# Last expert's sends behind the branch around the overflow part, its second products block by block, its last copy halved

## The chip, the cores and the metric

The kernel runs on one core of a Trainium2 chip. TensorE (PE) multiplies matrices, VectorE (DVE), ScalarE (ACT) and GpSimd (POOL) do the rest, SyncE (SP) issues most loads; POOL issues the indirect DMAs that scatter rows. The metric is the device time of one execution in microseconds (us). Before the change three runs took 419.87, 419.90 and 421.45 us, a median of 419.9 us.

## The reference, cut to what matters

```python
def _moe_ref(x, w_gate, w_output_gate, w1, w2):        # x: 3072 x 512, the output of the attention part
    e_idx = np.argmax(x @ w_gate, axis=1)              # one of 8 experts for each token
    ...                                                # gate_w: softmax; eom: sigmoid of x @ w_output_gate
    for e in range(E):
        mask = e_idx == e
        h = np.maximum(x[mask] @ w1[e], 0.0)           # 512 -> 1024
        ye = h @ w2[e]                                 # 1024 -> 512
        out[mask] = gate_w[mask, None] * eom[mask, e, None] * ye
```

Ahead of it stands a causal linear attention with decay (4 batches, 8 heads, 768 steps), whose output is x. All values are float32; the kernel splits each matrix into a high and a low part and does three products for one.

## The kernel before, in words

The first third (to about 150 us) computes the attention in chunks of 128 steps, picks each token's expert and scatters the tokens' rows, sorted by expert, into a buffer `srt` in device memory. Then the experts are worked through in order of their number of tokens. Each has a fixed room for tokens (`CAPS`, 448 down to 368). Tokens that do not fit, should there be any, are done at the end in the overflow part, which stands inside a branch, `tc.If(odd > 0)`. In the inputs at hand the count is zero and the branch jumps over it.

The work on experts is a loop over steps `s`, eight steps (slices of 128 of the 1024 hidden columns) to an expert; `NS` is 64. A step does the first product `mm1(s)` into a PSUM tile `h` (line 985; 12 matmuls, in one of four arms of a small branch, by the expert's size), then ACT and DVE make the two parts `hh` and `hl` of its relu (lines 994, 995), and the second product of the step before is added into four PSUM tiles `a`.

The last expert is different: its second product is turned round (`stage2_last`, line 1036), so that tokens lie on the partitions of the result. It has three blocks of tokens `tb` (128, 128 and 112), three matmuls of 512 columns for each block and step, and one PSUM tile for each block. When a block has all eight steps, `emit_last` (lines 1039 to 1049) copies it out of PSUM into `orow`, by ACT for blocks 0 and 2 and by DVE for block 1, and POOL sends it to the rows of `out` that `idl` names (`send`, line 215). `idl` holds the token numbers, made in step 61 by three small DVE operations.

The order of the instructions on each engine is the order in which the code is written (`manual_schedule`), up to `order_ctx.close()`. Behind it come the overflow part and the end of the program. Each of the five engines has its own copy of the branch: it loads the count `n_odd` (line 1117), compares and jumps (line 1143). Where the body is skipped, an engine runs a short other arm, which waits until its earlier work is complete and raises its semaphores by what the body would have raised. On POOL that arm waits for all its DMAs and then does one operation on the semaphores of the DMA queue, shown as INC_SWDGE_SEM. The end of the program (line 1254) is a chain of waits on SP, a DRAIN on each engine and a meeting of all engines.

Of the kernel before, what the change touches and what calls it, by code (L numbers as in the profile page):

```python
# [10 lines left out]
F32 = mybir.dt.float32  # L11
F32R = mybir.dt.float32r
BF16 = mybir.dt.bfloat16
I32 = mybir.dt.int32
# [19 lines left out]
def retention_moe_kernel(  # L34
# [14 lines left out]
    nc = tc.nc  # L49
    P = 128  # L50
    HP = P // 2
    B, H, S, D = q.shape
    E, DM, DF = w1.shape
    NT = B * S
# [4 lines left out]
    NF = DF // P  # L59
# [3 lines left out]
    NTB = math.ceil(CAPS[-1] / P)  # L63
# [3 lines left out]
    cpool = ctx.enter_context(tc.tile_pool(name="cpool", bufs=1))  # L67
    wpool = ctx.enter_context(tc.tile_pool(name="wpool", bufs=8))
    hpool = ctx.enter_context(tc.tile_pool(name="hpool", bufs=1))
# [8 lines left out]
    order_ctx = ExitStack()  # L78
    order_ctx.enter_context(tc.manual_schedule())

    def fill_up(pool, n):

        return pool.tile([P, n], F32, name="fill")
# [36 lines left out]
    iof = cpool.tile([P, E], F32, name="iof")  # L120
    ck = cpool.tile([P, E], F32, name="ck")
    arm = cpool.tile([P, E], I32, name="arm")
    fill_up(cpool, 24)

    def constants_first():

# [87 lines left out]
    def send(dst, idx, src, n):  # L214
        st = nc.gpsimd.indirect_dma_start(  # L215
            out=dst, out_offset=bass.IndirectOffsetOnAxis(ap=idx, axis=0),
            in_=src, in_offset=None, bounds_check=n - 1, oob_is_err=False)

        tc.declare_no_dep(st.ins, group="out", reason="rows are disjoint")
        tc.add_to_no_dep_group("out", st.ins)  # L220
# [17 lines left out]
    with ExitStack() as actx:  # L238
# [651 lines left out]
        run_head(12)  # L890
        split_low(NF - 1, None, nc.vector)

    with ExitStack() as mctx:
        mp = mctx.enter_context(tc.tile_pool(name="mp", bufs=2))
        NS = E * NF
# [140 lines left out]
                nc.tensor.matmul(accs[tb][0:w.stop - w.start], l[:, w], r[:, 1], start=(f == 0 and n == 0),  # L1036
                                 stop=(f == NF - 1 and n == 2))

        def emit_last(tb):
            n = min(P, CAPS[-1] - tb * P)  # L1040
            orow = mp.tile([P, DM], F32, name="orow", tag="orow", bufs=NTB)

            src = accs[tb][0:n].rearrange("p (dc a j) -> p dc a j", a=4, j=32)
            dst = orow[0:n].rearrange("p (a dc j) -> p dc a j", a=4, j=32)
            if tb % 2 == 0:
                nc.scalar.copy(dst, src)
            else:
                nc.vector.tensor_copy(dst, src)
            send(out, idl[0:n, tb:tb + 1], orow[0:n], NT)

        def load_idl(e):
            m = mp.tile([P, NTB], F32, name="idm", tag="idm", bufs=1)
# [1 line left out]
            return m  # L1054

        def round_idl(m):
            t = mp.tile([P, NTB], I32, name="idl", tag="idl", bufs=1)
            tmp = mp.tile([P, NTB], I32, name="tmpl", tag="tmpl", bufs=1)
            token_ids(t, m, slotl, ck[:, E - 2:E - 1], tmp, True)
            return t  # L1060

        arms = {}

# [20 lines left out]
        for s in range(NS + 1):  # L1084
            e, f = divmod(s, NF)
            if f == 0 and 1 <= e < E - 1:
                load_rank(e + 1)
            while loaded < min(NS, s + NF + 1):
                load_weights(loaded)
                loaded += 1  # L1090
            if f == 1 and e + 1 < E:
                load_x(e + 1)
            while split < min(NS, s + NF - 1):
                split_weights(split)
                split += 1
            first_mm = [lambda C: mm1(s, C)] if s < NS else []
            second_mm = [lambda C: mm2(s - 1, C)] if 1 <= s <= NS - NF else []
            if f == 0:
                if first_mm:
                    by_size(e, *first_mm)  # L1100
                if second_mm:
                    by_size(e - 1, *second_mm)
            else:
                by_size(e, *first_mm, *second_mm)
            if s < NS:
                relu1(s)
            if second_mm:
                finish(s - 1)
            if e == 0:
                if f >= 1:  # L1110
                    arms[f] = nc.values_load(arm[0:1, f - 1:f], engines=(mybir.EngineType.PE,), min_val=0, max_val=ARMS - 1)
            if NS - NF < s < NS - 1:
                for tb in range(NTB):
                    stage2_last(s - 1, tb)
            elif s == NS:

                odd = nc.values_load(n_odd[0:1, 0:1], min_val=0, max_val=NT + 1)
                for tb in range(2):
                    stage2_last(NS - 2, tb)
                for tb in range(NTB):  # L1120
                    if tb >= 2:
                        stage2_last(NS - 2, tb)
                    stage2_last(NS - 1, tb)
                    emit_last(tb)
            if e == 0:
                head_send(f)
            if f == NF - 1 and 1 <= e + 1 < E - 1:
                clear(e + 1)
            if e >= 1 and s < NS and f >= 1:
                for n in range(2 * f - 2, min(math.ceil(PASS[e - 1][1] / 32), 2 * f)):  # L1130
                    emit(e - 1, n)
            dc = f - (3 if e == 0 else 4)
            if 0 <= dc < NDC and e + 1 < E:
                prep_x(e + 1, dc)
            if s == NS - NF:
                idm = load_idl(E - 1)
            if s == NS - 3:
                idl = round_idl(idm)


    order_ctx.close()

    with tc.If(odd > 0):
        with ExitStack() as octx:
# [4 lines left out]
            def block(r0, e):  # L1149

                xo = op.tile([P, ROW], F32, name="xo", tag="xo")
                nc.sync.dma_start(xo, srt[ds(r0, P), :])
                oi = op.tile([P, 1], I32, name="oi", tag="oi")
                nc.vector.tensor_scalar(out=oi, in0=xo[:, P:P + 1].bitcast(I32), scalar1=-0.25, scalar2=0.25 * KEEP,
                                        op0=ALU.mult, op1=ALU.add)
                xf = op.tile([P, DM], F32, name="xf", tag="xf")
                nc.vector.tensor_copy(xf.rearrange("p (dc a j) -> p dc a j", a=4, j=32),
                                      xo.rearrange("p (a x) -> p a x", x=SEG)[:, :, 0:P].rearrange("p a (dc j) -> p dc a j", j=32))
                pt = psv.tile([P, NDC, P], F32, name="pt", tag="pt")
                for dc in range(NDC):  # L1160
                    nc.tensor.transpose(pt[:, dc], xf[:, dc * P:(dc + 1) * P], ident)
                xt = op.tile([P, NDC, P], F32, name="xto", tag="xto")
                nc.vector.tensor_copy(xt, pt)
                yo = op.tile([P, DM], F32, name="yo", tag="yo")
                ht = op.tile([P, NF, P], F32, name="ht", tag="ht")
                for fg in range(2):
                    wa = op.tile([P, NDC, 512], F32, name="wa", tag="wa")
                    for o in range(2):
                        nc.sync.dma_start(wa[o * HP:o * HP + HP], w1[ds(e, 1), o * DM // 2:(o + 1) * DM // 2, fg * 512:(fg + 1) * 512]
                                          .rearrange("z (dc p) f -> p (z dc) f", p=HP))  # L1170
                    ph = psv.tile([P, 4, P], F32, name="ph", tag="ph")
                    for j in range(4):
                        for dc in range(NDC):
                            nc.tensor.matmul(ph[:, j], wa[:, dc, j * P:(j + 1) * P], xt[:, dc],
                                             start=(dc == 0), stop=(dc == NDC - 1))
                    nc.scalar.activation(ht[:, fg * 4:fg * 4 + 4], ph, AF.Relu)
                po = psv.tile([P, DM], F32, name="po2", tag="po2")
                for fg in range(2):
                    wb = op.tile([P, 4, DM], F32, name="wb", tag="wb")
                    nc.sync.dma_start(wb, w2[ds(e, 1), fg * 512:(fg + 1) * 512, :].rearrange("o (j p) d -> p (o j) d", p=P))  # L1180
                    for j in range(4):
                        nc.tensor.matmul(po, ht[:, fg * 4 + j], wb[:, j], start=(fg == 0 and j == 0),
                                         stop=(fg == 1 and j == 3))
                nc.vector.tensor_copy(yo, po)
                nc.gpsimd.indirect_dma_start(
                    out=out, out_offset=bass.IndirectOffsetOnAxis(ap=oi, axis=0),
                    in_=yo, in_offset=None, bounds_check=NT - 1, oob_is_err=False)

            rows = oc.tile([P, 1], I32, name="rows")
            nc.gpsimd.iota(rows, pattern=[[0, 1]], base=0, channel_multiplier=1)  # L1190
# [17 lines left out]
            for r, cap in enumerate(CAPS + [TOP]):  # L1208
                nov = nc.values_load(over[0:1, r:r + 1], min_val=0, max_val=NT)
                with tc.If(nov > 0):  # L1210
                    e = nc.values_load(order[0:1, r:r + 1], engines=(ET.SP,), min_val=0, max_val=E - 1)
                    clear_from(endk[:, r:r + 1], 0)
                    with tc.For_i(0, nov, P) as t0:
                        block(e * REG + cap + t0, e)


# [42 lines left out]
```

## Time and profile before

| | us |
|---|---|
| median of three runs | 419.9 |
| the profiled execution's own time | 421.54 |
| span of the profiled execution, first to last instruction | 419.6 |
| TensorE busy | 404.4 |
| last matmul starts | 409.35 |
| last send starts on POOL | 411.11 |

The span is the stretch between the first and the last instruction of the trace; the execution's own time lies 1.95 us above it. Start times below count from the start of the span. Names such as POOLq or SPq mean an engine's sequencer, which takes instructions in order, waits on semaphores and jumps; POOL or DVE alone means the engine at work.

### The profile page before, as it was taken

The numbers are of one execution on the slowest core, as the hardware profiler recorded it, in microseconds if no ns is written. First come the engines' busy times: TensorE is split into PE (matmuls) and PEld (weight loads), VectorE is DVE, ScalarE is ACT, GpSimd is POOL, SyncE is SP. The second block draws the span as 40 slices with busy tenths as digits, with TensorE's granted clock in tenths as the row PEclk, the third lists the DMA queues.
The fourth block names the chain that finished last, engine by engine and source line by source line (L and its number), as shares of the span: only waits on it lengthen the run. The fifth ranks groups of instructions, "written<-read, shape, count | busy, mean of one in ns | idle before, by whom it ended". The sixth has DMA issues, their size and how long they took to land.

```text
span 419.6 us, 10492 instructions
## 1 busy us (share of the span) xinstructions
PE 404.4 (96%) x3611; PEld 378.3 (90%) x3611; DVE 222.8 (53%) x557; ACT 185.3 (44%) x360; POOL 257.3 (61%) x306
## 2 busy tenths in 40 slices
PE   7999999999999999999999999999999999999990
PEld 4878887888879999999999999999999999999880
DVE  3355667666687766744543553563555454553120
ACT  2366555555565325634533544443454454452110
POOL 3655664454587127883367777777786787876702
PEclk9899999999999999999999999999999999999996
DMA  8999788988744969797494588469459659620102
GB/s 187 256 240 244 214 232 220 252 204 220 203 141 154 248 147 269 222 211 191 141 224 140 148 200 207 155 180 232 136 172 237 176 168 208 214 75 28 47 3 75
DMA packets 130157, 75.75 MB, mean 181 GB/s; under 512 B 61748, under 2 KB 118216, under 8 KB 130064
## 3 DMA queue, kind: packets, MB, share of 16 engines
q1 hardware_dynamic: 122928, 59.38, 58.1%
q0 software_dynamic: 5904, 15.04, 10.3%
q8 instruction: 61, 1.00, 1.0%
q14 instruction: 32, 0.26, 0.2%
q10 hardware_dynamic: 1232, 0.06, 0.2%
HBM read 59.71 MB, written 15.30 MB: 179 GB/s over the span
## 4 chain that ended last, share of the span: by engine, by line
PE 79%; issue 5%; POOL 5%; DMA 5%; DVE 2%; ACT 1%; SPq 1%; POOLq 0%; ACTq 0%; DVEq 0%
PE h L985 29%; PE a L1008 27%; PE y L411 4%; PE s L393 4%; PE s L353 2%; PE st L418 2%; PE y L385 2%; POOL out_dram L215 2%; PE s L340 2%; PE s L522 1%; DMA qn<-in_q_dram 1%; PE s L622 1%; PE a L1036 1%; DMA raw<-in_moe_w_dram 1%; DMA srt<-row,pos 1%
## 5 line engine op out<-in xcount | busy, mean ns | idle before, releaser
L201 POOL TENSOR_TENSOR wlo<-raw,whi 128x512 fp32r<-128x512 f32 x56 | 74.9, 1338 | 44.3 <-ACT whi L193 27.1
L215 POOL DMA_INDIRECT out_dram<-ot,idi x85 | 84.7, 996 | 22.5 <-issue 17.7
L985 PE MATMUL h<-xh,whi 128*128 128x360 f32 (+5 forms) x256 | 84.3, 329 | 0.1
L985 PE MATMUL h<-xw,whi 128*128 128x360 f32 (+5 forms) x256 | 84.3, 329 | 0.0
L985 PE MATMUL h<-xh,wlo 128*128 128x360 f32 (+5 forms) x256 | 84.2, 329 | 0.0
L995 DVE SCALAR_TENSOR_TENSOR hl<-h,hh 128x192 fp32r<-128x192 f32 (+7 forms) x64 | 35.4, 554 | 82.8 <-ACT hh L994 81.2
L1008 PE MATMUL a<-hh,whi 128*128 128x392 f32 (+4 forms) x224 | 73.8, 329 | 0.0
L1008 PE MATMUL a<-hl,whi 128*128 128x392 f32 (+4 forms) x224 | 73.8, 329 | 0.0
L1008 PE MATMUL a<-hh,wlo 128*128 128x392 f32 (+4 forms) x224 | 73.5, 328 | 0.0
L994 ACT ACTIVATE hh<-h 128x192 fp32r<-128x192 f32 (+7 forms) x64 | 31.2, 488 | 73.5 <-PE h L985 73.5
L192 ACT CAST whi<-raw 128x512 fp32r<-128x512 f32 x64 | 39.6, 618 | 40.9 <-PE a L1008 31.1
L200 DVE TENSOR_TENSOR wlo<-raw,whi 128x512 fp32r<-128x512 f32 x60 | 42.4, 707 | 27.2 <-ACT whi L192 22.9
L985 PEld LDWEIGHTS h<-xh,whi 128*128 128x128 f32 x256 | 48.2, 188 | 0.9 <-issue 0.4
L985 PEld LDWEIGHTS h<-xw,whi 128*128 128x128 f32 x256 | 48.2, 188 | 0.6
L985 PEld LDWEIGHTS h<-xh,wlo 128*128 128x128 f32 x256 | 48.2, 188 | 0.2
L538 POOL DMA_INDIRECT srt<-row,pos x24 | 24.2, 1007 | 38.9 <-ACT row L529 31.2
L401 DVE TENSOR_TENSOR am<-s,mask 128x512 f32<-128x512 f32 x48 | 29.9, 684 | 30.6 <-PE s L393 28.5
L1008 PEld LDWEIGHTS a<-hl,whi 128*128 128x128 f32 x224 | 42.2, 188 | 0.3
L1008 PEld LDWEIGHTS a<-hh,wlo 128*128 128x128 f32 x224 | 42.2, 188 | 0.2
L1008 PEld LDWEIGHTS a<-hh,whi 128*128 128x128 f32 x224 | 42.2, 188 | 0.2
L193 ACT CAST whi<-raw 128x512 fp32r<-128x512 f32 x64 | 39.6, 618 | 1.1 <-DMA raw<-in_moe_w_dram 1.1
L927 ACT CAST xh<-xt 128x416 fp32r<-128x416 f32 (+2 forms) x28 | 15.1, 540 | 36.7 <-DVE xt L926 36.7
(201 smaller groups left out, 642.1 us busy)
## 6 DMA issues: line engine op xcount, KB each, us to landing
raw<-in_moe_w_dram SPq DMA_DIRECT2D x128, 128.0 KB, 4.8
raw<-in_moe_w_dram SPq DMA_DIRECT2D x64, 256.0 KB, 4.1
kn<-in_k_dram SPq DMA_DIRECT2D x24, 256.0 KB, 4.6
vn<-in_v_dram SPq DMA_DIRECT2D x24, 256.0 KB, 5.0
qn<-in_q_dram SPq DMA_DIRECT2D x10, 512.0 KB, 5.6
xl<-srt SPq DMA_DIRECT2D x12, 209.6 KB, 5.5
xl<-srt SPq DMA_DIRECT2D x8, 225.8 KB, 3.3
xl<-srt SPq DMA_DIRECT2D x8, 193.5 KB, 4.8
```

Of the source, the lines that this page charges most:

```text
L192: nc.scalar.copy(hi[:, 0], raw[:, 0])
L193: nc.scalar.copy(perm(hi), r2)
L200: (first or nc.vector).tensor_sub(lo[:, 0], raw[:, 0], hi[:, 0].bitcast(F32))
L201: (second or nc.gpsimd).tensor_sub(perm(lo), r2, perm(hi).bitcast(F32))
L215: st = nc.gpsimd.indirect_dma_start(out=dst, out_offset=bass.IndirectOffsetOnAxis(ap=idx, axis=0), in_=src, in_offset=None, bounds_check=n ...
L393: nc.tensor.matmul(sp[2 * (n % 2) + b][:, (2 * S_ + o) * P:(2 * S_ + o) * P + P], kt[n][rows(b), g], queries(n, g, b), start=True, stop=Tr ...
L401: nc.vector.tensor_tensor(out=a.rearrange("p s o t -> p (s o) t"), in0=sp[2 * (n % 2) + b].rearrange("p (x t) -> p x t", t=P), in1=mask.un ...
L538: s_ = nc.gpsimd.indirect_dma_start(out=srt, out_offset=bass.IndirectOffsetOnAxis(ap=rt.pop(("pos", i)), axis=0), in_=row.rearrange("p a x ...
L985: nc.tensor.matmul(ps[:, 0:C], l[:, 0, w], r[:, dc, 0:C], start=(n == 0), stop=(n == 3 * NDC - 1))
L994: nc.scalar.activation(hh, ps[:, 0:C], AF.Relu)
L995: nc.vector.scalar_tensor_tensor(out=hl, in0=ps[:, 0:C], scalar=0.0, in1=hh.bitcast(F32), op0=ALU.max, op1=ALU.subtract)
L1008: nc.tensor.matmul(accs[d][:, 0:C], l[:, 1, w], r[:, 0:C], start=(f == 0 and n == 0), stop=(f == NF - 1 and n == 2))
```

## The change

The three sends of the last expert move from in front of the branch to behind it: `emit_last` becomes `copy_last`, which only copies and puts the tile on a list `lasts`; the sends are written out after the overflow part. For that `orow` and `idl` move to pools that live to the end (`orow` to the three 2 KB buffers of tag `h0`, which the first expert's head used; `idl` to the constants, with the padding behind it cut from 24 to 16 words). The second products of step 61 no longer run between the first products of steps 62 and 63 but after the latter, together with those of steps 62 and 63, and all of one block of tokens before the next. The copy of the last block is split: ACT copies the first half of its columns, DVE the second. Block 0 stays with ACT and block 1 with DVE. The send inside the overflow part, which is skipped, is written with the helper.

```diff
@@ constants
+    idl = cpool.tile([P, NTB], I32, name="idl")
-    fill_up(cpool, 24)
+    fill_up(cpool, 16)
@@
-        def emit_last(tb):
+        def copy_last(tb):
             n = min(P, CAPS[-1] - tb * P)
-            orow = mp.tile([P, DM], F32, name="orow", tag="orow", bufs=NTB)
+            orow = hpool.tile([P, DM], F32, name="orow", tag="h0", bufs=3)
...
-            if tb % 2 == 0:
+            if tb == 0:
                 nc.scalar.copy(dst, src)
+            elif tb < NTB - 1:
+                nc.vector.tensor_copy(dst, src)
             else:
-                nc.vector.tensor_copy(dst, src)
-            send(out, idl[0:n, tb:tb + 1], orow[0:n], NT)
+                nc.scalar.copy(dst[:, 0:2], src[:, 0:2])
+                nc.vector.tensor_copy(dst[:, 2:4], src[:, 2:4])
+            lasts.append((orow, n))
@@ the loop over steps
-            if NS - NF < s < NS - 1:
+            if NS - NF < s < NS - 2:
                 for tb in range(NTB):
                     stage2_last(s - 1, tb)
             elif s == NS:
                 odd = nc.values_load(n_odd[0:1, 0:1], min_val=0, max_val=NT + 1)
-                for tb in range(2):
-                    stage2_last(NS - 2, tb)
                 for tb in range(NTB):
-                    if tb >= 2:
-                        stage2_last(NS - 2, tb)
-                    stage2_last(NS - 1, tb)
-                    emit_last(tb)
+                    for x in (NS - 3, NS - 2, NS - 1):
+                        stage2_last(x, tb)
+                    copy_last(tb)
@@
-    order_ctx.close()
     with tc.If(odd > 0):
...
+    for tb, (orow, n) in enumerate(lasts):
+        send(out, idl[0:n, tb:tb + 1], orow[0:n], NT)
+    order_ctx.close()
```

On POOL, at the end of its program, the order before was as follows (first the place of the branch, then, after the skipped body, the other arm and the end; `orow` and `idl` are the last expert's rows and token numbers, what stands in square brackets are the semaphores that a row waits for).

```order
L1117 TENSOR_LOAD n_odd [waits DVE_49]
L215 DMA out_dram<-orow,idl 3072x512 [waits DMASW0_49,DVE_49,Activation_49]
L215 DMA out_dram<-orow,idl 3072x512 [waits DMASW1_49,DVE_49]
L215 DMA out_dram<-orow,idl 3072x512 [waits DMASW2_49,Activation_49]
L1143 COMPARE_AND_BRANCH
...
L1143 ISA [waits Pool_49,Pool_sequencer_49,DMASW4_49,DMASW5_49,DMASW3_49,DMASW6_49,DMASW2_49,DMASW7_49,DMASW1_49,DMASW0_49]
L1143 UNCONDITIONAL_BRANCH
L1254 ISA [waits barrier_Pool_Activation_PE_DVE_SP_gather]
```

In the changed program the same place of POOL reads as follows.

```order
L1120 TENSOR_LOAD n_odd [waits DVE_49]
L1141 COMPARE_AND_BRANCH
...
L1141 ISA [waits Pool_49,Pool_sequencer_49,DMASW4_49,DMASW5_49,DMASW3_49,DMASW6_49,DMASW2_49,DMASW7_49,DMASW1_49,DMASW0_49]
L1141 UNCONDITIONAL_BRANCH
L216 DMA out_dram<-orow,idl 3072x512 [waits DMASW0_49,DVE_49,Activation_49]
L216 DMA out_dram<-orow,idl 3072x512 [waits DMASW1_49,DVE_49]
L216 DMA out_dram<-orow,idl 3072x512 [waits DMASW2_49,DVE_49]
L1254 UNCONDITIONAL_BRANCH
L1254 ISA [waits barrier_Pool_Activation_PE_DVE_SP_gather]
```

The three sends have moved past the branch and past the other arm's wait for the DMA queues; one jump to the program's end is new behind them.

On DVE, at the same place, the rows before are these (`hl` is the low part of a step's relu).

```order
L995 SCALAR_TENSOR_TENSOR hl<-h_2651,hh 128x368 [waits Activation_49]
L995 SCALAR_TENSOR_TENSOR hl<-h_2652,hh 128x368 [waits Activation_49]
L1117 TENSOR_LOAD n_odd [waits DVE_49]
L1048 COPY orow<-a_2646 128x4x4x32 [waits PE_49]
L1143 COMPARE_AND_BRANCH
```

And in the changed program:

```order
L997 SCALAR_TENSOR_TENSOR hl<-h_2653,hh 128x368 [waits Activation_49]
L1120 TENSOR_LOAD n_odd [waits DVE_49]
L1050 COPY orow<-a_2647 128x4x4x32 [waits PE_49]
L1053 COPY orow<-a_2648 112x2x4x32 [waits Activation_49]
L1141 COMPARE_AND_BRANCH
```

DVE has one copy more, a half of 256 columns, and it waits for ACT, not for PE: the two halves run one after the other.

## Rows read from the trace of the kernel before

**Rows 1.** The page, part 1: busy time, share and instructions of each engine.
```profile
PE 404.4 (96%) x3611; PEld 378.3 (90%) x3611; DVE 222.8 (53%) x557; ACT 185.3 (44%) x360; POOL 257.3 (61%) x306
```

**Rows 2.** Busy time by stretch: start:end, length, PE, PEld, DVE, ACT, POOL, clock, DMA share.
```profile
core 0: us, PE busy (x) PEld busy (x) DVE busy (x) ACT busy (x) POOL busy (x), PEclk, DMA share, GB/s
405.40:409.80 4.40, 4.34 (x20) 3.13 (x18) 1.23 (x2) 1.09 (x3) 0.97 (x1) 1.00 0.02 6
409.80:419.60 9.80, 0.00 (x0) 0.00 (x0) 0.00 (x0) 0.56 (x1) 1.96 (x2) 0.63 0.23 79
```

**Rows 3.** The chain of waits, end of the span: start, length, what.
```profile
396.65 0.97 POOL out_dram L215
...
409.84 0.62 POOL out_dram L215
410.46 0.65 issue
411.11 0.98 POOL out_dram L215
```

**Rows 4.** The timeline from 405 us: start, length, engine, operation [idle before, releaser].
```profile
405.61 0.48 ACT L994 ACTIVATE hh<-h 128x368 fp32r<-128x368 f32 x1 [3.52 <-PE h L985]
406.12 0.54 DVE L995 SCALAR_TENSOR_TENSOR hl<-h,hh 128x368 fp32r<-128x368 f32 x1 [3.46 <-ACT hh L994]
...
407.70 0.59 ACT L1046 COPY orow<-a 128x512 f32<-128x512 f32 x1 [1.61 <-PE a L1036]
...
408.39 0.69 DVE L1048 COPY orow<-a 128x512 f32<-128x512 f32 x1 [1.73 <-PE a L1036]
...
408.56 0.97 POOL L215 DMA_INDIRECT out_dram<-orow,idl  x1 [10.94 <-ACT orow L1046]
...
409.12 0.39 PE L1036 MATMUL a<-whi,hl 128*112 128x512 f32 x1
409.35 0.39 PE L1036 MATMUL a<-wlo,hh 128*112 128x512 f32 x1
409.78 0.58 ACT L1046 COPY orow<-a 112x512 f32<-112x512 f32 x1 [1.50 <-PE a L1036]
409.84 0.97 POOL L215 DMA_INDIRECT out_dram<-orow,idl  x1 [0.30 <-issue]
411.11 0.98 POOL L215 DMA_INDIRECT out_dram<-orow,idl  x1 [0.30 <-issue]
```

**Rows 5.** Instructions of the branch's line 1143: count, shortest/median/longest ns, first and last start.
```profile
L1143 POOLq EVENT_SEMAPHORE  x6: 17/30/571, 413.3 to 414.3; - x6
L1143 DVEq EVENT_SEMAPHORE  x2: 21/21/21, 411.3 to 411.4; - x2
L1143 ACTq EVENT_SEMAPHORE  x2: 17/17/17, 412.5 to 412.6; - x2
L1143 PEldq COMPARE_BRANCH  x1: 3473/3473/3473, 406.8 to 406.8; - x1
L1143 DVEq COMPARE_BRANCH  x1: 76/76/76, 408.4 to 408.4; - x1
L1143 ACTq COMPARE_BRANCH  x1: 54/54/54, 409.8 to 409.8; - x1
L1143 POOLq COMPARE_BRANCH  x1: 53/53/53, 410.4 to 410.4; - x1
L1143 POOLq INC_SWDGE_SEM  x1: 686/686/686, 415.9 to 415.9; - x1
```

**Rows 6.** The same line, 413.6 to 414.28 us alone: the wait for the third send.
```profile
L1143 POOLq EVENT_SEMAPHORE  x2: 43/307/571, 413.6 to 413.7; - x2
```

**Rows 7.** Instructions of the program's end, line 1254; the last row from 418.79 us alone.
```profile
L1254 SPq EVENT_SEMAPHORE  x14: 17/28/28, 416.5 to 419.5; - x14
L1254 POOLq DRAIN  x3: 46/103/2118, 416.6 to 419.3; - x3
L1254 SPq DRAIN  x3: 7/7/13, 417.3 to 419.0; - x3
...
L1254 POOLq EVENT_SEMAPHORE  x4: 17/17/17, 418.8 to 419.5; - x4
```

**Rows 8.** Copies and the like of 256 or 192 columns on ACT and DVE.
```profile
L442 ACT COPY lt<-misc x12: 368/405/405, 19.4 to 128.3; 128x256 f32<-128x256 f32 x12
L609 DVE SCALAR_TENSOR_TENSOR h<-y,h x7: 415/424/425, 131.8 to 149.7; 128x256 fp32r<-128x256 f32 x7
L995 DVE SCALAR_TENSOR_TENSOR hl<-h,hh 128x192 fp32r<-128x192 f32 x8 | 2.8, 353 | 1.3 <-ACT hh L994 1.1
```

**Rows 9.** The load of the count on POOL, line 1117.
```profile
L1117 POOLq TENSOR_LOAD <-n_odd x1: 506/506/506, 388.7 to 388.7; - x1
```

**Rows 10.** All sends into the output, whole span: time from issue to landing.
```profile
DMA to landing us min/median/max: 2.2/3.8/6.4
```

**Rows 11.** Jumps in the loop over steps, line 969, on PE's sequencer.
```profile
L969 PEldq COMPARE_BRANCH  x186: 65/176/2924, 171.4 to 402.1; - x186
```

More of the change, by code (lines that the diff above doesn't have):

```diff
@@ L891, in retention_moe_kernel @@
         split_low(NF - 1, None, nc.vector)
+    lasts = []
     with ExitStack() as mctx:
@@ L1056, in round_idl @@
         def round_idl(m):
-            t = mp.tile([P, NTB], I32, name="idl", tag="idl", bufs=1)
             tmp = mp.tile([P, NTB], I32, name="tmpl", tag="tmpl", bufs=1)
-            token_ids(t, m, slotl, ck[:, E - 2:E - 1], tmp, True)
-            return t
+            token_ids(idl, m, slotl, ck[:, E - 2:E - 1], tmp, True)
         arms = {}
@@ L1137, in retention_moe_kernel @@
             if s == NS - 3:
-                idl = round_idl(idm)
-    order_ctx.close()
+                round_idl(idm)
     with tc.If(odd > 0):
@@ L1184, in block @@
                 nc.vector.tensor_copy(yo, po)
-                nc.gpsimd.indirect_dma_start(
-                    out=out, out_offset=bass.IndirectOffsetOnAxis(ap=oi, axis=0),
-                    in_=yo, in_offset=None, bounds_check=NT - 1, oob_is_err=False)
+                send(out, oi, yo, NT)
             rows = oc.tile([P, 1], I32, name="rows")
```

## The prediction

> **What bounds the kernel now.** The page's first part comes first: TensorE is busy for 96% of the span [rows 1]. The stretches then show where that ends: to 409.8 us PE has no gap, and in the last 9.8 us it does nothing [rows 2]. The change adds and removes no matmul, so what it can win lies in those 9.8 us. The chain of waits ends in POOL's three sends and says nothing of what follows the last [rows 3]. The timeline shows the approach: three copies out of PSUM, three sends [rows 4]. The rest is found only in the instructions of the branch's line and of the program's end [rows 5 to 7], laid end to end:
>
> - The last matmul's result is ready at 409.78, where ACT's third copy starts; the copy ends at 410.36 [rows 4].
> - The third send could start 0.28 us later (that is the distance at the first: copy to 408.29, send at 408.56 [rows 4]), so at 410.64. It starts at 411.11, since POOL is still at the second; sends stand 1.28 apart. It ends at 412.09 [rows 4].
> - POOL's sequencer, behind the branch, waits for that send's landing until 413.7 + 0.57 = 414.3 [rows 6]. This is 2.2 us behind the send's end, and the shortest landing of any send into the output is 2.2 too [rows 10].
> - From that wait's end to the start of the operation on the queue's semaphores (415.9) pass 1.6 us, and it takes 0.69 [rows 5].
> - SP's chain of waits for the program's end can only start with it, 416.5 to 417.4 [rows 7]; POOL's DRAIN follows it, 416.6 + 2.12 = 418.75 [rows 7], and the meeting of the engines ends the span 0.84 us after that, at 419.59.
>
> So 5.3 us lie between the landing of the last byte and the end, and 1.6 + 0.69 + 2.12 of them are POOL's passage through the skipped branch, begun only after the landing.
>
> **The change part by part.** *Sends behind the branch.* POOL now meets the branch with nothing of the last expert in front of it. Its load of the count stands at 388.7 already [rows 9], since the sequencer runs ahead of the engine. After its jump an engine resumes 2.9 us later on DVE (408.4 to 411.3), 2.7 on ACT, 2.9 on POOL [rows 5]. The other arm must then wait for the sends of the expert before: the last ends at 397.62 [rows 3], lands 2.2 later, 399.8. Add 1.6 and 0.69: 402.1. Even with a further 2.1 us, should what the DRAIN waited for be work left over from that operation, POOL is free at 404.2. The first send needs the first copy, which comes at about 406.2 (below). This cover is POOL's idle time of 10.94 us ahead of the first send [rows 4]; if it were gone, the third send would still not be later as long as the first starts by 410.9 - 2 x 1.28 = 408.3.
>
> *Blocks one after the other.* The nine matmuls of step 61 move behind the first product of step 63. Their pitch is 0.23 us (409.12 to 409.35 [rows 4]), and PE's total stays. With six matmuls for block 0 ahead of the first that needs `hh` of step 63, 1.4 us, relu's two parts (0.48 + 0.54 [rows 4]) are covered exactly as before. The first block is complete 18 matmuls (4.15 us) before the end instead of nine: its copy runs 405.6 to 406.2, the second block's 407.7 to 408.4, and the sends start at 406.5 and 408.7. The second is over at 409.6, so the third no longer queues.
>
> *The last copy halved.* DVE's half waits for ACT's (the order shows it), so the halves add. ACT's takes 0.37 to 0.41 for 256 columns [rows 8]; I take 0.37, since the full copies stand at the short end too. No plain DVE copy of 256 columns is in the trace; other DVE work is 0.35 for 192 and 0.42 for 256 columns [rows 8], a full copy 0.69 [rows 4]. I take 0.42, the nearest row, and keep 0.35 to 0.69. With 0.03 between them (406.09 to 406.12, `hh` to `hl` [rows 4]) the third copy ends at 409.78 + 0.37 + 0.03 + 0.42 = 410.60, later by 0.24 than before. The send starts at 410.88 and ends at 411.86: earlier by 0.23, because the queue at POOL cost 0.47.
>
> *The end.* The landing follows at 411.86 + 2.2 = 414.05. From 3.8, the median over all sends [rows 10], I keep 1.6 us as an outer bound; those ran beside loads of weights, this one as before beside nothing. SP's chain takes 0.8 us (416.5 to 417.36 [rows 7]); only its second wait is for the last landing, so nearly all of it follows: 414.85. POOL's DRAIN starts at the send's end and takes 0.05 to 2.12 [rows 7]: at most 413.98, before SP. The other engines jump at 406.8 (PE, then 3.5 us), 409.8 and some 410.2, and are through by 413.4. The meeting adds 0.84: 415.7.
>
> *Nothing else.* `idl` and `orow` in other pools, the padding and the overflow's send run nowhere on the path: the count's branch is not taken, and the three `h0` buffers have lain idle since the first expert.
>
> **Sum.** 419.59 - 415.7 = 3.9 us of the span: 0.2 from the third send, 3.7 from the passage through the branch (1.6 + 0.69 + 2.12 go, SP's 0.8 now stands open, and small change between the rows). The profiled execution's own time is 421.54, 1.95 above its span; there the sum gives 417.6. The median of the runs shown is 1.64 lower; from it, 419.9 - 3.9 = 416.0 us.
>
> **A rule beside a row.** POOL's first DRAIN at the end stands at 2118 ns [rows 7]. The Trainium skill ("VectorE: DVE Perf Modes", section "The DRAIN you can't avoid") calls the boilerplate DRAIN of every engine a constant of about 12 ns; this trace disagrees by its row, and by the page rival C below could not happen, while the sum would stay at 416.0 because SP is last either way.
>
> **The rivals.**
>
> A. *The forecast*, 416.0, chance 0.72.
>
> B. *The new jump costs again.* Behind the third send stands a jump to the program's end that was not there. If it holds POOL up as the branch did, 2.9 us from about 410.6, POOL is at its DRAIN at 413.5, through at 415.6, the span ends at 416.5, time 416.8; with a second stop of 1.6 us, 418.4. For it: each of DVE, ACT and POOL took 2.7 to 2.9 us at its jump [rows 5]. Against: the other arm of each engine ends in a jump to the end too, and DVE's two steps (411.3 and 411.4) are followed by its DRAIN at 411.5 without a stop. Chance 0.10. The Trainium skill ("Runtime: NRT & Kernel Launch", section "Instruction fetch mechanics") says that a taken branch stalls when its target is outside the two pages at hand; by that rule this jump, over nothing, is free unless a page ends there.
>
> C. *POOL's DRAIN waits for the landing.* Then 414.05 + 2.12 + 0.84 = 417.0, time 417.3. For it: the long DRAIN came in the one place where sends had just gone out. Against: they had landed 2.3 us before it began. Chance 0.08.
>
> D. *PE runs dry between steps 62 and 63.* Nothing stands between their two small branches now. For it: the longest jump there is 2.92 us [rows 11]. Against: the median is 0.18, and PE's sequencer runs ahead; the last of these jumps, at 402.1 [rows 11], stands behind a product that is ready only at 405.61, where `hh` starts [rows 4], 3.5 us later. Price from 0 to 2.9, so up to 418.9. Chance 0.04.
>
> E. *The join holds the sends back: slower.* If they started only when DVE, which jumps last, is through its other arm, the first would start at about 413.8 instead of 406.5, the third end at 413.8 + 2 x 1.28 + 0.98 = 417.3, land at 419.5, and the span end at 421.2: time 421.5, with C's DRAIN 422.8. It decides from a first send after 412.2. For it: the sends stand behind a place where every engine raises its semaphores. Against: in the order they wait for copies and for their queue alone. Chance 0.03.
>
> F. *The change does not reach the end*: POOL's time there belongs to the program's end, not to the branch, 419.7. Against: the 0.69 stands on the branch's line [rows 5]. Chance 0.03.
>
> **How the numbers follow.** A measurement of this kernel can tell about 0.5% (2.1 us) from no change. Faster by more means below 417.8: A, C, B but for its long form, half of D: 0.88. Slower by more, above 422.0: part of E, and a disturbed measurement (one of the runs shown is 1.5 above the others): 0.03. The rest, 0.09, is within. The range: A's low end is 415.0 (DVE's half at 0.35, and SP's 0.8 gone but for a wait or two); upward it takes in B's and C's short forms and stops at 417.7.
>
> **What would show it.** In the profile after: on POOL the operation on the semaphores before the first `orow` send, near 402; the first send at 406.5, the third at 410.9; DVE's half copy directly behind ACT's, at 410.2; SP's chain starting early and its second wait ending at 414; POOL's DRAIN over before 414; the end at 415.7. A DRAIN ending with the landing or later shows C, a gap on POOL between third send and DRAIN shows B, a gap on PE at 401 to 404 shows D, sends after 412 show E. If PE is not dense to 409.8, the sum is wrong from its first line.

## The result and the profile after

The changed kernel takes 417.56 us (median of 7 runs, 416.88 to 418.77) against 421.3 for the kernel before in the same comparison (7 runs, 419.87 to 422.82). The ratio is 0.9914, with a 95% interval from 0.9892 to 0.9935: 3.7 us faster, and the interval does not reach 1. Forecast were 3.9 us less, from a start of 419.9, so 416.0; the time is 1.56 us above that and inside the range, and 1.4 us of the 1.56 are the start, which is 421.3 in this comparison. The profiled execution took 416.88 us, 4.66 less than the one before, and its span is 414.9, 4.7 less.

First the page's part 1 of the kernel after, where [rows 1] stood: busy time, share of the span, instructions.

```profile
PE 403.5 (97%) x3611; PEld 378.5 (91%) x3611; DVE 223.2 (54%) x558; ACT 184.8 (45%) x360; POOL 257.1 (62%) x306
```

The counts are the same but for one DVE instruction more, the second half of the last copy. Next the busy time by stretch of the kernel after, cut where its last matmul ends, to set against [rows 2]; columns as there.

```profile
core 0: us, PE busy (x) PEld busy (x) DVE busy (x) ACT busy (x) POOL busy (x), PEclk, DMA share, GB/s
403.50:408.40 4.90, 4.84 (x21) 3.46 (x20) 0.69 (x1) 0.61 (x2) 1.94 (x2) 1.00 0.16 57
408.40:414.90 6.50, 0.00 (x0) 0.00 (x0) 0.42 (x1) 0.35 (x1) 0.98 (x1) 0.68 0.23 78
```

PE is dense to the last matmul at a full clock, as before; what follows is 6.5 us instead of 9.8. Two of the three sends now lie beside PE's work. The timeline of the kernel after shows them (start, length, engine, line, operation; in brackets the idle time ahead and what ended it), as [rows 4] did for before.

```profile
402.12 0.48 ACT L996 ACTIVATE hh<-h 128x368 fp32r<-128x368 f32 x1 [1.44 <-PE h L987]
...
404.20 0.58 ACT L1048 COPY orow<-a 128x512 f32<-128x512 f32 x1 [1.61 <-PE a L1038]
405.06 0.97 POOL L216 DMA_INDIRECT out_dram<-orow,idl  x1 [8.85 <-ACT orow L1048]
406.29 0.69 DVE L1050 COPY orow<-a 128x512 f32<-128x512 f32 x1 [3.12 <-PE a L1038]
407.26 0.97 POOL L216 DMA_INDIRECT out_dram<-orow,idl  x1 [1.22 <-DVE orow L1050]
407.94 0.40 PE L1038 MATMUL a<-wlo,hh 128*112 128x512 f32 x1
408.38 0.37 ACT L1052 COPY orow<-a 112x256 f32<-112x256 f32 x1 [3.58 <-PE a L1038]
408.78 0.42 DVE L1053 COPY orow<-a 112x256 f32<-112x256 f32 x1 [1.80 <-ACT orow L1052]
409.48 0.98 POOL L216 DMA_INDIRECT out_dram<-orow,idl  x1 [1.25 <-DVE orow L1053]
```

Each send waits for its copy and none for the send ahead of it. The last matmul starts at 407.94, where [rows 4] has 409.35; those 1.41 us came in ahead of the last matmul, in a stretch that the change reorders without adding or removing a matmul (more on this below). From here on times are therefore counted from the start of the last matmul, "+2.52" say, and the stretch from there to the end of the span is called the tail. The third send ends at 409.48 + 0.98, that is +2.52; before it was 411.11 + 0.98 - 409.35 = +2.74.

The branch's line of the kernel after (count, shortest/median/longest ns, first and last start) answers to [rows 5].

```profile
L1141 POOLq EVENT_SEMAPHORE  x6: 17/30/43, 390.4 to 397.4; - x6
L1141 ACTq EVENT_SEMAPHORE  x2: 17/17/17, 411.6 to 411.7; - x2
L1141 DVEq EVENT_SEMAPHORE  x2: 21/21/21, 411.9 to 412.0; - x2
L1141 POOLq COMPARE_BRANCH  x1: 53/53/53, 387.9 to 387.9; - x1
L1141 POOLq INC_SWDGE_SEM  x1: 636/636/636, 397.5 to 397.5; - x1
...
L1141 DVEq COMPARE_BRANCH  x1: 76/76/76, 408.8 to 408.8; - x1
```

POOL jumps at 387.9, goes on at 390.4, and the operation on the semaphores is done at 398.1, seven us ahead of the first send. DVE is the last to jump, resumes three us later, and is through at 412.0, before the landing. Then the program's end, as [rows 7]; the last row is POOL's DRAINs from 413.56 us alone.

```profile
L1254 SPq EVENT_SEMAPHORE  x14: 17/28/14378, 398.1 to 414.8; - x14
L1254 POOLq EVENT_SEMAPHORE  x4: 17/17/17, 413.6 to 414.8; - x4
L1254 POOLq DRAIN  x3: 46/246/4303, 409.2 to 414.6; - x3
L1254 SPq DRAIN  x3: 7/7/13, 413.1 to 413.8; - x3
...
L1254 POOLq DRAIN  x2: 46/146/246, 414.1 to 414.6; - x2
```

What SP's long wait is for stands in the view of waits on SP of the kernel after (line, releaser, us in total, times, longest).

```profile
SPq L1254 <- DMA out_dram<-orow,idl: 14.4, 1, 14.4
```

SP waits 14,378 ns, from 398.12 to 412.49, for the third send's landing, 2.03 us behind that send's end. Its chain is through at 413.22, 0.73 later. But POOL's DRAIN, 4303 ns long, ends only at 413.55, 1.06 us behind the landing, and POOL's first EVENT_SEMAPHORE of the meeting stands right behind it, at 413.6. From there to the end pass 1.33 us, not 0.84. The tail is thus 2.52 + 2.03 + 1.06 + 1.33 = 6.94 us, and it was 10.23.

### The profile page after: what moved, and what is told of

It reads as the page before. It is cut to its first block, busy times and chain, and to the rows that moved or that the text cites. A ratio compares the mean times of both kernels' runs of the same rounds, so it can differ in the third digit from the quotient of the medians.

```text
span 414.9 us, 10493 instructions
## 1 busy us (share of the span) xinstructions
PE 403.5 (97%) x3611; PEld 378.5 (91%) x3611; DVE 223.2 (54%) x558; ACT 184.8 (45%) x360; POOL 257.1 (62%) x306
## 4 chain that ended last, share of the span: by engine, by line
PE 82%; DMA 5%; issue 5%; DVE 2%; POOL 2%; ACT 2%; SPq 1%; POOLq 0%; ACTq 0%; DVEq 0%
PE h L987 28%; PE a L1010 27%; PE s L394 6%; PE y L412 5%; DMA out_dram<-ot,idi 3%; PE s L354 2%; PE s L523 2%; PE y L386 2%; PE st L419 2%; PE s L341 2%; DMA qn<-in_q_dram 1%; PE misc L438 1%; DMA raw<-in_moe_w_dram 1%; PE s L623 1%; ACT row L530 1%
```

## The experiments

All tails in one table, each from one profile, in us from the start of the last matmul; "INC" is POOL's operation on the queue's semaphores, "meeting" the time from the end of POOL's long DRAIN to the end of the span. Times are medians, ratios are to the kernel before in the same comparison.

| kernel | third send ends | INC starts | POOL's DRAIN ends | meeting | tail | time | ratio, 95% interval |
|---|---|---|---|---|---|---|---|
| before | 2.74 | 6.56 | 9.40 | 0.83 | 10.23 | 421.3 | |
| before again (e10) | 2.74 | 6.54 | 9.38 | 0.84 | 10.22 | 421.37, one run | |
| after | 2.52 | -10.47 | 5.61 | 1.33 | 6.94 | 417.56 | 0.9914, 0.9892 to 0.9935 |
| e1 sends behind the branch alone | 2.74 | -10.47 | 6.01 | 1.33 | 7.34 | 417.54 | 0.9925, 0.9901 to 0.995 |
| e2 order and halves alone | 2.52 | 4.71 | 7.55 | 0.83 | 8.38 | 417.76 | 0.9927, 0.9901 to 0.9952 |
| e3 before without the branch | 2.74 | none | 5.83 | 0.83 | 6.66 | 416.22 | 0.9892, 0.9867 to 0.9918 |
| e4 after without the branch | 2.52 | none | 5.62 | 0.83 | 6.45 | 416.13 | 0.9882, 0.9854 to 0.991 |
| e5 last copy whole | 2.27 | -16.4 | 5.38 | 1.33 | 6.71 | 426.38 | 0.9915, 0.9883 to 0.9948 |
| e7 after again | 2.52 | -16.3 | 5.61 | 1.33 | 6.94 | 427.18 | 0.993, 0.9899 to 0.9961 |
| e6 late loads | 2.52 | -13.7 | 7.37 | 1.33 | 8.70 | 426.89, one run | |
| e8 before, POOL's code moved on | 2.74 | 5.06 | 7.90 | 0.84 | 8.74 | 419.03 | 0.9967, 0.9948 to 0.9985 |
| e9 copy whole, code moved on | 2.27 | -10.46 | 5.37 | 0.86 | 6.23 | 416.29 | 0.9911, 0.9876 to 0.9946 |

The kernel before took 420.71 beside e1 to e4, 430.42 beside e5 to e7 (a chip on which every kernel ran 2% longer; only their tails and ratios are compared) and 420.57 beside e8 to e10.

**One half of the change each.** e1 is the kernel before with the sends alone behind the branch; order and copies stay, the pools of `orow` and `idl` are those of the changed kernel.

```diff
-            send(out, idl[0:n, tb:tb + 1], orow[0:n], NT)
+            lasts.append((orow, n))
...
-    order_ctx.close()
     with tc.If(odd > 0):
...
+    for tb, (orow, n) in enumerate(lasts):
+        send(out, idl[0:n, tb:tb + 1], orow[0:n], NT)
+    order_ctx.close()
```

> The kernel before with one part of the change: the three sends stand behind the branch; order of the blocks and whole copies as before. Theory (POOL's passage through the skipped branch stood behind the last landing): from the last matmul's start to the end of the span 10.23 us before, 6.94 in the changed kernel; here the third copy ends 0.24 earlier than in the changed kernel but the sends queue at POOL again, so the third send ends 2.74 us after the last matmul's start as before, and the rest is the changed kernel's 4.42: 7.2 us in all, 3.1 us faster than before, ratio about 0.993. Rival (the gain is the order of the blocks, which frees POOL's queue): 10.2 us, ratio 1.000.

The instructions of the branch's line and of the end in e1, POOL's sequencer alone:

```profile
L1141 POOLq INC_SWDGE_SEM  x1: 640/640/640, 398.8 to 398.8; - x1
...
L1253 POOLq DRAIN  x3: 46/247/4956, 410.3 to 416.3; - x3
L1253 POOLq EVENT_SEMAPHORE  x4: 17/17/17, 415.3 to 416.5; - x4
```

INC is early here too, the tail 7.34, 2.89 us shorter than before. The third send is where it was, +2.74, so all of this lies behind it. How much of it is the passage and how much the 1.6 us in front of INC, e1 alone does not say. The DRAIN is longer by 0.65 us than after's, because it starts 0.25 us sooner (the sequencer hands the third send on as soon as its copy is over, here a whole one, while the second is still running) and ends 0.40 later. That it ends with the landing is tested in e6.

e2 is the other half: the kernel after with the sends back in front of the branch (and the send inside the overflow part written out as before).

```diff
-            lasts.append((orow, n))
+            send(out, idl[0:n, tb:tb + 1], orow[0:n], NT)
...
+    order_ctx.close()
     with tc.If(odd > 0):
...
-    for tb, (orow, n) in enumerate(lasts):
-        send(out, idl[0:n, tb:tb + 1], orow[0:n], NT)
-    order_ctx.close()
```

> The other part alone: second products block by block, last copy halved, idl and orow in the new pools, but the sends in front of the branch as before. Theory: only the third send's 0.23 us, so 10.0 us from the last matmul's start to the end, ratio about 0.9995. Rival (the order makes the gain): about 7 us, ratio 0.992.

It was expected to gain the third send's 0.2 and gained 1.85. The same rows in e2:

```profile
L1142 POOLq EVENT_SEMAPHORE  x6: 17/30/170, 412.9 to 413.5; - x6
L1142 POOLq INC_SWDGE_SEM  x1: 695/695/695, 413.6 to 413.6; - x1
...
L1253 POOLq DRAIN  x3: 46/103/2118, 414.3 to 417.0; - x3
L1253 POOLq EVENT_SEMAPHORE  x4: 17/17/17, 416.5 to 417.1; - x4
```

The last wait starts at 413.5 and INC at 413.57: there is no gap. In [rows 5] the last wait starts at 414.3 and INC at 415.9. INC (0.69) and DRAIN (2.118) cost what they cost before. So the passage does not need the 1.6 us that the prediction put to it; e2 lost them without anything in its edit that was meant to do so. POOL's program is seven instructions different there; a stop that depends on where the code lies would do that. e8 and e10 test it.

**The place of the code.** e8 is the kernel before with 32 small instructions for POOL inside the skipped body, which never run. They move all that stands behind on POOL by 32 places.

```diff
             rows = oc.tile([P, 1], I32, name="rows")
             nc.gpsimd.iota(rows, pattern=[[0, 1]], base=0, channel_multiplier=1)
+            pad = oc.tile([P, 1], I32, name="pad")
+            for _ in range(32):
+                nc.gpsimd.memset(pad, 0)
```

> The kernel before with 32 tiny memsets on POOL added inside the overflow part, which is skipped: nothing of them runs, but POOL's other arm and the program's end stand 32 places later in its code. With the order alone changed (sends in front of the branch) the 1.6 us between the last landing's wait and POOL's operation on the semaphores were gone and that code stood 7 places later. Theory now (those 1.6 us are a stop for code at a place where POOL's code crosses a boundary, an accident of where the arm stands): the gap falls from 1.56 to under 0.1 us, 8.6 us from the last matmul's start to the end instead of 10.23, ratio to before about 0.996. Rival (the gap belongs to POOL's engine after three sends in a row): 10.2 us, ratio 1.000.

e10 is the kernel before, unchanged, beside it.

> The kernel before once more, for its profile. If the 1.6 us gap on POOL belongs to the place of the code, it is there again within 0.2 us, and 10.2 us lie between the last matmul's start and the end; if it was a chance of that one execution, it is not.

POOL's waits and INC of e8:

```profile
L1143 POOLq EVENT_SEMAPHORE  x6: 17/30/554, 411.2 to 412.1; - x6
...
L1143 POOLq INC_SWDGE_SEM  x1: 695/695/695, 412.2 to 412.2; - x1
```

and of e10:

```profile
L1143 POOLq EVENT_SEMAPHORE  x6: 17/30/552, 413.5 to 414.5; - x6
...
L1143 POOLq INC_SWDGE_SEM  x1: 690/690/690, 415.8 to 415.8; - x1
```

In e8 INC follows the last wait at once, and the tail is 8.74, shorter by 1.49; the medians differ by 1.54. In e10 the stop is back. It is no fixed time behind the landing, either: in e10 the waits end 0.17 us later than in before (414.52 against 414.35), the gap is 1.25 instead of 1.56, and INC starts 5.49 us after POOL's jump in the one and 5.51 in the other. So in the kernel before POOL's instruction at this place is not to be had until 5.5 us after the jump, and moving the code by 32 places takes this away. The DMA queues have packets of the kind "instruction", those on queue q14 of 8,192 bytes. From the last waits on, these are what moved, in this order, in before (414.15 to 419.5 us), in e10 (414.1 to 419.4) and in e8 (411.95 to 415.85): queue, packets, MB, share.

```profile
q14 instruction: 2, 0.02, 1.1%
q14 instruction: 2, 0.02, 1.1%
q14 instruction: 1, 0.01, 0.7%
```

In before such a packet starts about 1.0 us behind each of the jumps of DVE, ACT and POOL (409.43, 410.83, 411.40), and a second one 2.7 to 2.9 us behind each first. The second that goes with POOL's jump is on its way from 414.19 to 414.74, and INC starts 1.17 us after its end (1.13 in e10). One more packet starts 0.68 us behind INC's start (0.69 in e10). In e8 the second packet is there too (412.02 to 412.43), but INC starts while it is on its way, and none follows to the end of the span. So where the stop is, INC starts only after a packet of code has come in, and where the padding has moved the code it starts without that. A row does not name the engine that a packet is for; that INC stood in the code which this packet brought is the reading that fits all three profiles. The Trainium skill ("Runtime: NRT & Kernel Launch", section "Instruction fetch mechanics") says that a taken branch whose target lies outside the two pages at hand stalls for a fetch. The trace agrees for the jump itself (2.9 us on POOL [rows 5], 2.6 in after). For going on from one block of code into the next the section calls the cost mostly hidden; the gap of 1.56 us in before and 1.25 in e10 was not.

**Without the branch.** e3 and e4 are before and after with the whole overflow part deleted; they leave that part of the computation out, which the inputs at hand do not reach.

```diff
-    with tc.If(odd > 0):
-        ...
```

> The kernel before without the overflow part (no branch and no body; the count is still loaded). Theory: the passage is gone, so as with the sends behind the branch: third send ends 2.74 us after the last matmul's start, 4.4 more to the end, 7.2 us; ratio about 0.993. Rival (those microseconds belong to the program's end, whatever stands before it): 10.2 us, ratio 1.000.

> The changed kernel without the overflow part. Theory (in the changed kernel the branch costs nothing any more, it lies beside the last matmuls): 6.94 us from the last matmul's start to the end, within 0.3, ratio to before the same as the changed kernel's 0.991. Rival (the late jumps of ACT and DVE, through at 412.1 of 414.9, or the new jump of POOL still hold the end up): 0.5 to 1 us less, ratio 0.989 to 0.990.

POOL's end in e3:

```profile
L1181 POOLq DRAIN  x3: 46/109/4780, 408.9 to 414.2; - x3
L1181 POOLq EVENT_SEMAPHORE  x4: 17/17/17, 413.7 to 414.4; - x4
```

and in e4:

```profile
L1183 POOLq DRAIN  x3: 46/109/4317, 409.9 to 414.8; - x3
L1183 POOLq EVENT_SEMAPHORE  x4: 17/17/17, 414.3 to 414.9; - x4
```

With no branch on the way the kernel before has a tail of 6.66: the branch, with the stop in front of INC, cost it 3.57. The kernel after has 6.45, and the difference of the two is 0.21, the third send. Against after's 6.94 the branch still costs 0.49, all of it in the meeting (0.83 here, 1.33 there); POOL's DRAIN ends at +5.61 and +5.62. So POOL's passage is hidden wholly, as forecast, and what is left stands elsewhere.

**The last copy.** e5 is the kernel after with the third copy left whole on ACT; e7 is the kernel after beside it.

```diff
-            if tb == 0:
+            if tb % 2 == 0:
                 nc.scalar.copy(dst, src)
-            elif tb < NTB - 1:
-                nc.vector.tensor_copy(dst, src)
             else:
-                nc.scalar.copy(dst[:, 0:2], src[:, 0:2])
-                nc.vector.tensor_copy(dst[:, 2:4], src[:, 2:4])
+                nc.vector.tensor_copy(dst, src)
```

> The changed kernel with the last copy whole on ACT instead of two halves one after the other. Theory: the halves take 0.37 + 0.03 + 0.42 = 0.83 us, the whole copy 0.585 (the copies of blocks 0 and 2 before); nothing queues at POOL, so the third send starts 0.24 us earlier and the end with it: 6.7 us from the last matmul's start to the end instead of 6.94, ratio to before 0.0006 below the changed kernel's. Rival (the end is set by something that does not follow the third send): 6.94.

> The changed kernel once more, on the same chip as the two beside it: 6.9 us from the last matmul's start to the end, within 0.2, and a ratio to before of about 0.991; how far the stretch ahead of the last expert moves from run to run is read from where the last matmul starts (409.35 before, 407.94 in the changed kernel's profile).

The timeline of e5:

```profile
417.84 0.58 ACT L1048 COPY orow<-a 112x512 f32<-112x512 f32 x1 [3.59 <-PE a L1038]
418.70 0.98 POOL L216 DMA_INDIRECT out_dram<-orow,idl  x1 [1.00 <-ACT orow L1048]
```

One copy of 0.58 takes the place of 0.37 + 0.03 + 0.42 = 0.82; the third send ends 0.25 us sooner and the tail is 6.71 against 6.94. Once the sends no longer queue, halving the copy over two engines that wait for each other is a loss, a small one; the medians (426.38 and 427.18, with overlapping intervals) cannot tell it.

**What POOL's DRAIN waits for.** e6 is the kernel after with four loads of weights into free tiles, issued by SP while the last matmuls run, so that they fill the DMA queues while the third send is on its way. The loads are not part of the computation.

```diff
                     copy_last(tb)
+                for g in range(4):
+                    junk = mp.tile([P, CAPS[0]], F32, name="junk", tag=("hh", "hl")[g % 2], bufs=3)
+                    nc.sync.dma_start(junk, w2[0, g * P:(g + 1) * P, 0:CAPS[0]])
```

> The changed kernel with four loads of 229 KB added on SP, into buffers that the last expert's matmuls free at about 1 to 2 us before the last matmul ends; nothing reads them. They keep the DMA engines busy while the last sends land. In the changed kernel POOL's DRAIN ends 3.09 us after the third send's end and 1.06 us after its landing. If the DRAIN waits for the landing, it moves with it: a landing 1 to 2 us later, a DRAIN that ends about 1 us after that. If it is POOL's own remaining work, it ends 3.1 us after the third send's end, whenever the landing is.

The timeline of e6, at the loads and the send:

```profile
415.50 1.77 SPq L1127 DMA_DIRECT2D junk<-in_moe_w_dram  x4
...
418.00 0.98 POOL L216 DMA_INDIRECT out_dram<-orow,idl  x1 [1.25 <-DVE orow L1053]
```

and its busy time by stretch (columns as above; DMA share last but one), then the end:

```profile
416.80:420.80 4.00, 0.06 (x1) 0.00 (x0) 0.42 (x1) 0.37 (x1) 0.98 (x1) 0.86 0.90 293
```

```profile
L1257 POOLq EVENT_SEMAPHORE  x4: 17/17/17, 423.9 to 425.1; - x4
L1257 POOLq DRAIN  x3: 46/246/6062, 417.8 to 424.9; - x3
```

The DMA engines are 90% busy where the send goes out. Its last packet is 1.68 us later than in after (+5.88 against +4.19), and POOL's DRAIN, 6062 ns long, ends 1.76 later, while the send itself ends at +2.52 in both. So the DRAIN waits for what has been sent, not for a remainder of POOL's own work. SP's DRAIN moved along, since SP waits for the same landing; its wait in e6 is this row, of 422.55 to 422.8 us alone.

```profile
L1257 SPq EVENT_SEMAPHORE  x1: 204/204/204, 422.6 to 422.6; - x1
```

So a rival is that POOL is released with SP. The distances decide it: in after, e1, e3, e4, e5, e6, e7 and e9 POOL's DRAIN ends 1.055 or 1.056 us behind the end of SP's wait for the landing (422.77 to 423.83 in e6), while from the start of SP's second DRAIN it is 0.40 in six of them, 0.47 in e3 and 0.53 in e4. POOL follows the landing and not SP's DRAIN.

**The best of both.** e9 is e5 with the 32 unused instructions of e8: the whole copy, and POOL's code moved on.

```diff
+            for _ in range(32):
+                nc.gpsimd.memset(pad, 0)
```

> The changed kernel with the last copy whole on ACT and the same 32 memsets in the skipped part. In the changed kernel and in every one with the sends behind the branch the meeting at the end takes 1.33 us after POOL's DRAIN, in the others 0.83; the extra 0.5 stands between two neighbours of POOL's end. If it is the same kind of boundary: 6.2 us from the last matmul's start to the end (6.71 with the whole copy alone, less 0.5), ratio to before about 0.990. Rival (the meeting is longer because the sends stand right in front of it): 6.7 us.

The end of e9:

```profile
L1254 POOLq DRAIN  x3: 46/109/4314, 409.3 to 414.1; - x3
L1254 POOLq EVENT_SEMAPHORE  x4: 17/17/17, 413.6 to 414.3; - x4
```

The meeting is back at 0.86 us. In after its second DRAIN takes 246 ns and starts at 414.12, 0.43 behind the semaphore ahead of it; here it takes 109 and stands close behind. So the 0.5 us hung on the code's place as well. The packets of code say the same: in after, e1, e5, e6 and e7 one starts 0.68 to 0.70 us behind the start of that second DRAIN (414.82 in after), as behind INC in before; in e9, e3 and e4 none does. The tail is 6.23, the shortest here, 0.71 under after's; the median, 416.29, is the lowest of the kernels with the overflow part, but its interval covers after's ratio, so the time alone does not settle which is faster.

## Why the prediction was right, step by step

- **PE dense to the end, blocks in their order, sends apart**: as forecast. The forecast put the third send's end 2.51 us behind the last matmul (411.86 against 409.35); it is 2.52. The halves took 0.372 + 0.03 + 0.424; the operation that was bounded by [rows 8] lies at the value taken.
- **POOL's passage hidden**: as forecast, and e4 shows that nothing of it is left on the path. INC ends at 398.10 against 402.1: POOL's wait for the last ordinary send is over 1.2 us behind that send's end (396.21 to 397.42), not 2.2, the 1.6 us in front of INC are not there, and this stretch lies 1.4 us earlier in the profile.
- **The landing**: 2.03 against 2.2. The 2.2 was right as it was read from [rows 6]; that [rows 10] has a 2.2 too is chance, since it counts from a send's start. Counted so, the last send of the kernel after takes 3.0 us.
- **The other rivals**: B's jump costs nothing that shows: POOL's DRAIN starts at 409.25, which is +1.30, and in e4, without the branch, at +1.30 too. D's gap is not there (PE is busy for all of 399.0 to 403.5). Against E, the first send starts at 405.06 and DVE is through its arm only at 412.0.
- **"POOL's DRAIN ... at most 413.98, before SP"** failed. It is rival C's mechanism, with a smaller price: the DRAIN waits for the landing and ends 1.06 us behind it, not 2.12. SP's chain is hidden under it, so the price over SP is 0.33 us (413.55 against 413.22), not the rival's 1.3. The row of before, 2118 ns, could not have given this: there the DRAIN stood behind INC. The Trainium skill ("VectorE: DVE Perf Modes", section "The DRAIN you can't avoid") calls the boilerplate DRAIN on all engines a constant of about 12 ns; PE, ACT, DVE and SP agree with their 7 to 17 ns at the end of before and after, but POOL's longest was 2118, 4303 and 6062 ns in before, after and e6, so for POOL the measurement decides against it.
- **"The meeting adds 0.84"** failed by 0.49 in the kernel after (1.33). e9 and e4 bring 0.83 to 0.86 back, one by the code's place, one by another end of the program.
- **"1.6 + 0.69 + 2.12 of them are POOL's passage"** is the term that was right in the sum and wrong in its cause. The 1.6 goes, but not because the passage is hidden: e8 takes it away with the sends left in front of the branch. Without either stop of this kind the tails are 8.74 (e8) and 6.94 - 0.49 = 6.45. So of the 3.29 us that the tail lost, 0.22 are the third send's, some 2.1 the passage's (INC, and what the DRAIN behind it took beyond its wait for the landing), and the remaining 1.0 is what the code's place gave (1.49) less what it took (0.49). The third send's share is 0.21 in the pair of e3 and e4, and 0.40 in the pair of e1 and after, so the parts are good to about 0.2. Set against e8, the tail of the changed kernel is only 1.80 shorter.

The sum of the steps against the forecast, from the third send's end to the end of the span: forecast 2.2 + 0.8 + 0.84 = 3.84, measured 2.03 + 1.06 + 1.33 = 4.42. That 3.7 us between the medians comes so near to the forecast 3.9 is in part luck: the tail gave 3.29, the other 0.45 lies outside it, and the place of the code, which the forecast did not know of, gave 1.0 of the 3.29. The rest of the profiled difference, 1.41 us, lies ahead of the last matmul, and nothing shows it to be the change: among the kernels outside the slower chip's comparison the last matmul starts at 407.15 to 409.35 in those that have before's order there (before, e1, e3, e8, e10) and at 407.94 to 408.86 in those with after's (after, e2, e4, e9). A profiled span alone would have given the change 4.7 us.

Open: the medians of e2, e3 and e4 lie 0.8 to 1.1 us further below before's than their tails explain (e2: 2.95 against 1.85), those of e1 and e8 only 0.3 and 0.05. The intervals reach about 1 us to each side, so little of this is clear of noise. Whether that is the stretch ahead, which varies by as much from one profile to the next, or something that the edits do there, was not settled. Nor was it tested why one place of the code costs 1.5 us and another 0.5. It would fit that in before the packet of code came just then, while the second one behind POOL's jump in after came at 391.0 to 391.5, 22 us before the meeting.

## What to carry to other kernels

What a program waits for at its end belongs behind its last branch: with the sends ahead of it, as in the kernel before, POOL's steps in the skipped arm came after the last landing, and with them behind it the arm ran while POOL was idle. Before a gap between two instructions on a sequencer is put to the instruction that follows, move the code by some unused instructions in a body that is skipped: if the gap goes, it was a matter of place, and an unrelated edit can bring it back. To judge a change of the last microseconds, count from the last instruction that the change leaves alone, since the span of the kernel before alone went from 417.0 to 420.4 us over the runs of one comparison (beside e8 to e10).

## What was not expected of the hardware

- A DRAIN on POOL at the program's end is long: 2118 ns right behind the operation on the queue's semaphores (before, e2, e8, e10), and with an indirect send on its way until 1.06 us after that send's landing as SP sees it, 6062 ns in e6.
- An engine that has jumped over a large body can stop a second time, several instructions behind the target: POOL until 5.5 us after its jump in before and e10, 1.1 to 1.2 us after a packet of code had come; 32 unused instructions removed the stop (tail 10.23 to 8.74).
- From the jump over the body to the next instruction an engine took 2.6 us on POOL (387.9 to 390.4) and 3.2 on ACT (408.4 to 411.6) in after, and 3.9 to 4.3 on ACT, DVE and SP in e6, where the added loads filled the DMA queues.
